# A one-core Nyström attention and SiLU layer: the written-out order of all compute pieces is replaced, and 80 PSUM copies change engine

## The chip, the core and the metric

The kernel runs on one core of a Trainium2 chip. A core has four engines that compute, each with its own queue of instructions that it works off strictly in order: TensorE (PE, matrix products into PSUM; its weight loads are listed apart as PEld), VectorE (DVE), ScalarE (ACT) and GpSimd (POOL). A fifth queue, SyncE (SP), only issues transfers here. An instruction that waits for a semaphore holds up everything behind it in its own queue, and nothing else. Transfers are issued from SP, POOL and, at the very end, ACT, and share the core's 16 DMA engines.

The metric is the time of one execution in microseconds. Three timed runs of the kernel before gave 241.28, 240.32 and 242.66 us, median 241.28.

## The reference

```python
def _attn_ref(q, k, v):                       # (8, 8, 576, 64) each
    q_lm = q.reshape(B, H, 32, 18, D).mean(axis=3)
    k_lm = k.reshape(B, H, 32, 18, D).mean(axis=3)
    A  = sm(q, k_lm)                          # softmax(a @ b.T / 8)
    Bm = sm(q_lm, k_lm)
    C  = sm(q_lm, k)
    Z = Bm.T / (norm_1(Bm) * norm_inf(Bm) + 1e-06)
    for _ in range(6):
        Z = 2 * Z - Z @ Bm @ Z
    return A @ Z @ C @ v

x = attn_out.transpose(0, 2, 1, 3).reshape(4608, 512)
h = x @ w_in                                  # 512 -> 2048
return (h * sigmoid(h)) @ w_out               # 2048 -> 512
```

Landmarks are means over groups of 18 tokens. The inverse of the 32 x 32 matrix Bm is found by six Newton steps, which follow one another. The result is float32.

## The kernel before, in words

The eight batches are worked on one after the other, with two or three of them under way at once. All work is cut into 1,565 named pieces; `name.b` is the piece of batch `b`. A piece is one function that emits one or several instructions on one engine:

- **Loads.** `ldk`, `ld`, `ldv` bring q, k and v; `wi` and `wo` the two weight matrices. The first batch's q and k come through SP and are cast by `kc...ACT` and `kc...DVE`; all other loads go through POOL (lines 398 to 432).
- **Transposed q and k.** For batches 0 to 2 PE transposes (`tr`, line 523) and a copy `trc` takes the block out of PSUM (lines 344 on ACT, 346 on DVE). From batch 3 on SP transposes by DMA (`xt`, line 547). A landmark sum is `lms` on PE for two batches, and `lra` to `lrd` on DVE (line 582) later.
- **Attention.** `sb` and `pb` give Bm; a chain of small DVE pieces and PE products makes the six Newton steps: `ns` (PE), `nsd` (DVE, line 717), `fb` (DVE, line 692), numbered by step and, for batch 0, by half. `A` and `C` are the big score products, each of which fills four PSUM banks; `Ax`, `Cx` are their exponentials on ACT (lines 749, 794), `S`, `Ln`, `Rs`, `etn` the normalisation. `ct` transposes C (by PE with the copy `ctc` for batches 0 and 1, then by DMA on SP, line 821); `cv` multiplies it by v, `wc` scales it (DVE, line 852), `zt` and its copy `ztc` apply Z, and `m0` to `m3` with the copies `mc` carry it through w_in.
- **First layer.** `h0` to `h15` and `hx0`, `hx8` on PE, `g` and `gx` the SiLU on ACT (lines 919, 942).
- **Second layer.** Every tile of 256 tokens is done by seven products of half size instead of eight. A tile's number follows the `@`: 5000 + 100 b + 0 or 20, and 5340, 5740 for the tokens that `gx` collects over four batches. `ss0` to `ss3` (DVE, line 1007) make the sums that the seven products `p1` to `p7` read; `c1`, `u2`, `c5`, `c21` copy a product out of PSUM (ACT or DVE), `c11`, `c12`, `c22` add a second one to it on DVE (line 1042). The first 256 tokens are done plainly (`o`, `oc`). The result lies in one of six staging tiles `ost` until four stores `os` (line 984) have carried it out; the copy that writes a staging tile anew waits for their landing.
- **Filler.** `*n` stands for n matmuls on zeros, 64 in all, in the first 28 us.

What sets the order is a text, `SEQUENCE`, at the head of the file. `Plan.run` goes through its words and each piece is emitted in that place; a word may carry the engine (`c1@5300.0/ACT`) and, behind `<`, the transfer after which it may start (`ld100.5<xt10.4`: those loads wait for that DMA transposition). So the text fixes each engine's queue, and PSUM banks are handed out in the order of the words, from the pieces that freed them. Semaphore waits between queues follow from the data. Nothing is reordered afterwards.

Of the kernel before, what the change touches and what calls it, by code (L numbers as in the profile page):

```python
# [25 lines left out]
Cx10.0 Cx11.0 Cx00.0 pbs.0 pbr.0 bmx.0 bmt.0 csb.0 n1.0 nrm.0 tr09.1 lms000.1 lms006.1 S10.0
lms0012.1 lms010.1 bbd.0 trc09.1/DVE stz.0 f0.0 stf0.0 stf1.0 fb00.0 lms016.1 Ln10.0 S00.0 Ln00.0
fb01.0 lms0112.1 lmc0.1/DVE S01.0 ns00.0 nsd00.0 Ln01.0 S11.0 ns01.0 Ln11.0 nsd01.0 fb11.0 ctm00.0
ctc00.0/DVE tr05.1 trc05.1/ACT tr00.1 trc00.1/ACT Rs1.0 Rs0.0 ns11.0 nsd11.0 fb10.0 fb21.0 tr19.1
trc19.1/DVE ltr0.1 lms100.1 lms106.1 ns10.0 nsd10.0 lms1012.1 tr014.1 lms110.1 lms116.1  # L30
trc014.1/DVE ns21.0 tr114.1 lmT0.1/ACT wi1a wi0a wi1b1 wi1b0 wi3b0 wi3a lms1112.1 lmc1.1/ACT
tr10.1 trc10.1/ACT tr15.1 *2 ltr1.1 lmT1.1/ACT fb20.0 nsd21.0 etn1.0 trc15.1/DVE ns20.0 fb31.0 *3
ns31.0 ctm10.0 trc114.1/ACT etn0.0 nsd31.0 sb.1 pb.1 *1 A.1 Ax01.1 Ax00.1 nsd20.0 fb30.0 pbs.1
wrc.0 *1 ns30.0 nsd30.0 ctc10.0/DVE fb40.0 pbr.1 fb41.0 bmx.1 bmt.1 wi3b1 Ax11.1 Ax10.1 *5 C.1
Cx00.1 Cx11.1 Cx01.1 *1 ns40.0 nsd40.0 ns41.0 nsd41.0 fb50.0 fb51.0 cv0.0 cv1.0 wc.0 S01.1 Ln01.1
ns50.0 nsd50.0 *2 ns51.0 bbd.1 nsd51.0 zbd.0 S11.1 Ln11.1 S00.1 Ln00.1 wi2b0 wi2b1 wi2a ldv0.1
ldv1.1 *5 zt.0 ztc.0/DVE S10.1 ctm00.1 ctc00.1/DVE Rs0.1 Ln10.1 Cx10.1 *2 m1.0 mc11.0/ACT
mc10.0/DVE m0.0 f0.1 mc01.0/DVE mc00.0/ACT *1 ctm10.1 ctc10.1/DVE Rs1.1 csb.1 *1 h4.0 n1.1 m3.0
nrm.1 stz.1 stf0.1 mc31.0/DVE fb00.1 g4.0 mc30.0/DVE h2.0 g2.0 h6.0 g6.0 h0.0 g0.0 h3.0 ns00.1
wrc.1 nsd00.1 fb10.1 h5.0 g5.0 m2.0 mc21.0/ACT mc20.0/DVE *1 h13.0 g13.0 ns10.1 nsd10.1 fb20.1  # L40
h15.0 hx0.0 g15.0 ns20.1 nsd20.1 fb30.1 h9.0 g9.0 h11.0 g11.0 etn0.1 ns30.1 nsd30.1 fb40.1 hx8.0
gx8.0 g3.0 h8.0 h12.0 g12.0 etn1.1 ns40.1 nsd40.1 fb50.1 gx0.0 h10.0 g10.0 ld1.2 tr15.2
trc15.2/DVE h14.0 g14.0 ns50.1 nsd50.1 zbd.1 ldv2.1 cv0.1 wc.1 tr114.2 trc114.2/DVE tr19.2
trc19.2/DVE zt.1 g8.0 ztc.1/ACT tr10.2 trc10.2/DVE lra1.2 h7.0 g7.0 m3.1 mc31.1/ACT mc30.1/ACT
m1.1 mc11.1/DVE mc10.1/ACT h1.0 g1.0 ld0.2 tr00.2 lrb1.2 tr09.2 tr014.2 trc014.2/DVE tr05.2
trc05.2/DVE trc09.2/DVE lrc1.2 trc00.2/ACT h12.1 g12.1 h7.1 g7.1 h15.1 m2.1 mc20.1/ACT m0.1
mc00.1/ACT mc21.1/ACT mc01.1/ACT wo0 o0@5001.0 h14.1 g14.1 g15.1 o0@5000.0 fold lrd1.2 lra0.2
lrb0.2 lrc0.2 lrd0.2 h11.1 g11.1 ltr0.2 ltr1.2 lmT1.2/DVE lmT0.2/ACT ss00@5020.0 ss10@5020.0
ss20@5020.0 ss30@5020.0 wo1 h5.1 o1@5000.0 sb.2 pb.2 pbs.2 pbr.2 bmx.2 bmt.2 wo2 wt00 bbd.2 h8.1
h3.1 o1@5001.0 o2@5000.0 wo3 o2@5001.0 wt01 g8.1 csb.2 o3@5001.0 oc@5001.0/ACT g3.1 g5.1 n1.2  # L50
nrm.2 stz.2 o3@5000.0 hx8.1 f0.2 gx8.1 h0.1 g0.1 oc@5000.0/ACT h2.1 h10.1 g10.1 h4.1 h1.1 g2.1
g1.1 wt11 wt21 stf0.2 fb00.2 ns00.2 h13.1 g13.1 wt31 nsd00.2 fb10.2 wt10 wt20 wt30 p1@5020.0
c1@5020.0/ACT ns10.2 nsd10.2 fb20.2 h9.1 h6.1 g4.1 g9.1 g6.1 ss00@5100.0 p5@5020.0 c5@5020.0/DVE
hx0.1 gx0.1 ss10@5100.0 l1done.0 C.2 Cx00.2 Cx10.2 p6@5020.0 u2@5020.0/DVE ld100.3 ld101.3 ld110.3
ld111.3 ldv1.3 xt10.3<ldv1.3 xt11.3<ldv1.3 ns20.2 nsd20.2 ss20@5100.0 p3@5020.0 c12@5020.0
# [198 lines left out]
def kernel(  # L254
# [9 lines left out]
    nc = tc.nc  # L264
# [86 lines left out]
    A = P.add  # L351
# [817 lines left out]
```

## Time and profile before

| | |
|---|---|
| profiled execution | 242.09 us |
| its span (first to last instruction) | 240.4 us |
| granted TensorE clock, mean | 0.998 |
| PE busy | 231.0 us in 2,948 matmuls |
| DVE busy | 181.7 us in 505 instructions |
| ACT busy | 182.9 us in 436 instructions |
| DMA moved | 37.73 MB, mean 157 GB/s |
| start of the first product on real data | 5.32 us |
| start of the last DVE copy | 236.50 us, 0.42 us long |

The profiled execution took 0.81 us more than the median of the three timed runs. Engines' busy shares are sums over the whole span; a group's mean time is the length of one instruction, and since an engine overlaps the end of one with the start of the next, its step from start to start is shorter (a first-layer SiLU on ACT is 625 ns long and follows the last one after 477 ns).

### The profile page before, as it was taken

The page shows a single profiled execution, that of the slowest core. Times are in us where ns is not written, and L with a number is a line of the kernel's source. Part 1 is how long each engine was busy: PE and PEld are TensorE (multiplying, and loading weights), DVE is VectorE, ACT ScalarE, POOL GpSimd, SP SyncE. Part 2 cuts the span into 40 slices and gives each one's busy share as a digit, 9 for nine tenths or more (in the row PEclk, how much of TensorE's full clock was granted, in tenths as well). Part 3 has the DMA queues.
Part 4 walks back from the last instruction along what each step waited for, and adds up shares of the span by engine and source line. Part 5 has one row for each costly group of instructions (what it writes and reads, how often), then busy time and mean ns, then how long its engine had stood idle before and what let it go on. Part 6 is the DMA issues. An engine that isn't in the chain of part 4 may idle for free.

```text
span 240.4 us, 7520 instructions
## 1 busy us (share of the span) xinstructions
PE 231.0 (96%) x2948; PEld 164.6 (68%) x2948; DVE 181.7 (76%) x505; ACT 182.9 (76%) x436; POOL 49.4 (21%) x89
## 2 busy tenths in 40 slices
PE   6999999999999989999789999999999999999993
PEld 4977556457876645788668655767876665789882
DVE  2679989898998579858699968759898475348762
ACT  3689999989889988998355899999779788634100
POOL 0936842140154006203060352000000000000000
PEclk9999999999999999999999999999999999999999
DMA  6999999999999996998999999992524421012334
GB/s 255 252 205 192 204 211 206 209 205 200 151 176 191 220 216 125 181 190 159 192 166 208 194 186 244 140 209 56 111 60 119 114 57 35 0 44 74 92 108 127
DMA packets 56164, 37.73 MB, mean 157 GB/s; under 512 B 37056, under 2 KB 47552, under 8 KB 56128
## 3 DMA queue, kind: packets, MB, share of 16 engines
q0 software_dynamic: 15168, 17.18, 44.5%
q1 hardware_dynamic: 40144, 19.12, 36.6%
q10 hardware_dynamic: 816, 0.95, 1.4%
q8 instruction: 23, 0.38, 0.6%
q14 instruction: 13, 0.11, 0.2%
HBM read 36.70 MB, written 9.44 MB: 192 GB/s over the span
## 4 chain that ended last, share of the span: by engine, by line
PE 84%; ACT 7%; DMA 2%; SPq 2%; DVE 2%; issue 1%; ACTq 0%; DVEq 0%
PE ps L334 81%; PE ps L523 3%; ACT gm L919 2%; DMA gm<-in_k_dram 2%; ACT L919 1%; SPq L821 1%; ACT L1122 1%; ACT gx L942 1%; SPq L984 1%; ACT m L344 1%; DMA out_dram<-ost 1%; PE ps L809 1%; ACT et L749 1%; DVE ss L1007 0%; DVE ost L1042 0%
## 5 line engine op out<-in xcount | busy, mean ns | idle before, releaser
L919 ACT ACTIVATE gm<-ps 128x512 f16<-128x512 f32 x128 | 68.7, 625 | 8.4 <-PE ps L334 7.9
L334 PE MATMUL ps<-etn,m 128*128 128x512 bf16 (+1 forms) x512 | 72.0, 286 | 0.2
L334 PEld LDWEIGHTS <-gm 128*128 128x128 f16 x512 | 48.5, 98 | 12.7 <-issue 1.6
L334 PE MATMUL ps<-w_out_sb,gm 128*128 128x256 f16 (+1 forms) x392 | 53.1, 281 | 0.1
L334 PEld LDWEIGHTS <-ss 128*128 128x128 f16 x408 | 39.2, 98 | 10.8 <-issue 2.8
L334 PEld LDWEIGHTS <-m 128*128 128x128 bf16 x512 | 31.1, 98 | 20.1 <-issue 2.1
L334 PE MATMUL ps<-wt,ss 128*128 128x256 f16 x272 | 34.6, 273 | 0.4 <-DVE st L717 0.4
L1042 DVE TENSOR_TENSOR ost<-ost,ps 128x256 f32<-128x256 f32 x51 | 21.0, 417 | 15.8 <-PE ps L334 8.1
L344 ACT COPY ost<-ps 128x256 f32<-128x256 f32 (+1 forms) x45 | 17.2, 388 | 12.3 <-PE ps L334 9.8
L344 ACT CAST m<-ps 128x512 bf16<-128x512 f32 x36 | 19.4, 613 | 1.8 <-PE ps L334 1.6
L415 POOL DMA_DIRECT2D v<-in_v_dram x24 | 14.5, 616 | 27.6 <-PE ps L334 25.2
L346 DVE CAST m<-ps 128x512 bf16<-128x512 f32 x28 | 18.3, 685 | 2.2 <-PE ps L334 1.9
L717 DVE SCALAR_TENSOR_TENSOR st<-st,ps 128x128 bf16<-128x128 bf16 (+2 forms) x54 | 13.6, 257 | 8.1 <-PE ps L334 4.8
L334 PE MATMUL ps<-w_out_sb,ss 128*128 128x256 f16 x136 | 17.5, 273 | 1.4 <-ACT ost L344 1.4
L398 POOL DMA_DIRECT2D qk<-in_k_dram x20 | 10.5, 546 | 35.6 <-DMA qT<-qk 17.7
L334 PE MATMUL ps<-wt,gm 128*128 128x256 f16 x120 | 15.6, 273 | 0.0
L759 ACT ACTIVATE ln<-ps 128x288 f32<-128x288 f32 x32 | 12.4, 415 | 3.7 <-PE ps L334 3.2
L692 DVE TENSOR_TENSOR fb<-st,hmask 128x256 bf16<-128x256 bf16 (+1 forms) x54 | 14.4, 272 | 1.0
L398 POOL DMA_DIRECT2D qk<-in_q_dram x20 | 10.5, 543 | 21.3 <-issue 11.9
L794 ACT ACTIVATE ce<-ps 128x288 bf16<-128x288 f32 x32 | 13.0, 424 | 2.5 <-PE ps L334 2.3
L1007 DVE TENSOR_TENSOR ss<-gm 128x1024 f16<-128x1024 f16 x15 | 10.2, 686 | 5.2 <-ACT gm L919 5.2
L749 ACT ACTIVATE et<-ps 128x288 bf16<-128x288 f32 x32 | 11.1, 423 | 2.9 <-PE ps L334 2.9
(93 smaller groups left out, 345.0 us busy)
## 6 DMA issues: line engine op xcount, KB each, us to landing
out_dram<-ost SPq DMA_DIRECT2D x128, 64.0 KB, 2.2
v<-in_v_dram POOLq DMA_DIRECT2D x24, 192.0 KB, 7.3
qk<-in_k_dram POOLq DMA_DIRECT2D x20, 144.0 KB, 5.9
qk<-in_q_dram POOLq DMA_DIRECT2D x20, 144.0 KB, 6.8
w_out_sb<-in_moe_w_out_dram POOLq DMA_DIRECT2D x4, 512.0 KB, 15.0
gm<-in_k_dram SPq DMA_DIRECT2D x2, 576.0 KB, 4.2
gm<-in_q_dram SPq DMA_DIRECT2D x2, 576.0 KB, 6.5
qk<-in_q_dram POOLq DMA_DIRECT2D x2, 576.0 KB, 8.2
```

The costliest lines, as they stand in the source:

```text
L334: nc.tensor.matmul(out=out_ap, lhsT=lhsT, rhs=rhs, start=start, stop=stop, skip_group_check=True)
L344: nc.scalar.copy(out=out, in_=in_)
L346: nc.vector.tensor_copy(out=out, in_=in_)
L398: lambda e, t=t, g=g, h=h, src=src: nc.gpsimd.dma_start(out=qk_r[b % 2][64 * h:64 * h + 64, t, g].rearrange("p j d -> p (j d)"), in_=src[b ...
L415: lambda e, a=a: nc.gpsimd.dma_start(out=v_r[b % 2][a * L:(a + 1) * L, :, :], in_=v[b].rearrange("h (l a x) d -> a l h (x d)", l=L, a=VA)[ ...
L692: nc.vector.tensor_tensor(out=fb[it % 2][:, g0:g1], in0=bc(sr[it % 3][:, g0:g1, 0:L], 4, 2), in1=bc(hmask, n, 1), op=OP.mult), [o], 14.5 + ...
L717: nc.vector.scalar_tensor_tensor(out=s2[:, g0:g1, lo:SW], in0=s[:, g0:g1, lo:SW], scalar=2.0, in1=ps[:, 0:NG * SW].rearrange("p (g x) -> p ...
L749: lambda e, g=g, et=et, c=c: nc.scalar.activation(out=et[:, c], in_=bank(me["A"], 2 * g + c)[:, 0:HS], func=AF.Exp, scale=sc / J),
L759: lambda e, g=g, c=c, ln=ln: nc.scalar.activation(out=ln[:, c], in_=bank(me["S", g, c])[:, 0:HS], func=AF.Ln),
L794: nc.scalar.activation(out=ce[:, :, 0:VP].rearrange("p (i c) (a l) -> p c a i l", c=2, a=VA)[:, c], in_=bank(me["C"], 2 * g + c)[:, 0:HS]. ...
L919: lambda e, dc=dc, cell=cell: nc.scalar.activation(out=gm[:, dc, :], in_=bank(cell["o"]), func=AF.Silu),
L1042: nc.vector.tensor_tensor(out=out_, in0=x, in1=y, op=OP.add)
```

## The change

`SEQUENCE` is written anew. It holds the same 1,565 pieces and the same 64 filler matmuls. The transfers of SP, of POOL and of ACT stand in the same order as before within their queues, and the words behind `<` are the same. All compute pieces may stand elsewhere, and 80 of the copies that either DVE or ACT can do have changed engine: 45 from ACT to DVE (13 `mc`, 13 of `c1`, `c5` and `c21`, 6 `u2`, 5 `lmT`, 3 `trc`, 3 `ztc`, one `lmc`, one `oc`) and 35 the other way (11 of `c1`, `c5` and `c21`, 9 `mc`, 5 `trc`, 3 `u2`, 2 each of `lmc`, `lmT` and `ztc`, one `ctc`). Since transfers wait for the last word that wrote their data, the compute pieces that some transfers wait for differ as well. Two lines outside the text let a store hand back its instruction; nothing uses it in this order. The diff, cut to the places that are spoken of below (first the old text, then the new one):

```diff
-ldk10 ldk11 ldk00 ldk01 const ident kc10ACT kc10DVE kj10 *15 lms100.0 tr15.0 tr10.0 trc10.0/DVE
...
-lmT0.0/ACT *6 sb.0 pb.0 trc014.0/DVE trc09.0/DVE A.0 Ax01.0 Ax00.0 Ax10.0 Ax11.0 *5 C.0 Cx01.0
...
-etn0.2 lmT0.3/ACT sb.3 c12@5100.0 c21@5020.0/ACT p7@5100.0 pb.3 pbs.3 pbr.3 fb50.2 A.3 Ax11.3
...
-zbd.2 zt.2 ztc.2/ACT S10.3 Ln10.3 p4@5100.0 Cx11.3 ss00@5120.0 c11@5100.0 os@5100.0 ss10@5120.0
...
-ns50.3 nsd50.3 zbd.3 h11.2 g11.2 h13.2 h3.2 cv0.3 wc.3 g4.2 g13.2 g3.2 etn1.3 zt.3 ztc.3/DVE
...
-ss20@5300.0 pbs.5 Ln00.4 p4@5220.0 p5@5300.0 c21@5220.0/ACT c5@5300.0/ACT Rs0.4 pbr.5 ss30@5300.0
-bmx.5 nsd00.4 fb10.4 wrc.4 p6@5300.0 u2@5300.0/ACT p3@5300.0 csb.5 ns10.4 n1.5 ss00@5320.0 etn1.4
...
-Ax10.5 Ax00.5 c1@5320.0/ACT p5@5320.0 ss10@5320.0 ns30.4 ss20@5320.0 ss00@5340.0 f0.5 stf0.5
-p4@5300.0 Ax01.5 Ax11.5 S11.5 Ln11.5 c21@5300.0/ACT p6@5320.0 u2@5320.0/ACT nsd30.4 fb40.4 ns40.4
...
+ldk10 const ident kc10DVE *1 kc10ACT ldk11 kc11DVE *1 ldk00 ldk01 kc11ACT *2 kc00ACT kc01ACT *1
...
+trc19.0/DVE tr15.0 trc15.0/ACT A.0 Ax01.0 ltr0.0 lmT0.0/DVE *1 Ax11.0 Ax10.0 *1 ld1.2 sb.0 pb.0
...
+etn1.0 ctc10.0/ACT lmc1.1/DVE nsd20.0 trc19.1/DVE trc10.1/ACT nsd11.0 trc014.1/DVE *1 ltr1.1
...
+Rs1.3 mc31.2/DVE c12@5100.0 etn1.3 ldv2.4<xt00.3 u2@5120.0/ACT os@5100.0 bbd.3 Cx01.3 os@5101.0
...
+ns50.3 h1.2 h3.2 cv0.3 ldv1.5 nsd50.3 g1.2 g14.2 etn0.3 wc.3 zbd.3 h0.2 hx0.2 zt.3 h2.2 g0.2 g3.2
...
+p5@5300.0 S00.4 Ln00.4 nsd00.4 ss20@5320.0 p6@5300.0 pbs.5 fb10.4 c5@5300.0/DVE ns10.4 nsd10.4
+p2@5220.0 fb20.4 ss00@5340.0 c1@5320.0/ACT ns20.4 S01.4 ct1.4<ldv1.5 p3@5300.0 c21@5220.0/ACT
...
-        {"SP": nc.sync, "ACT": nc.scalar}[e].dma_start(
+        return {"SP": nc.sync, "ACT": nc.scalar}[e].dma_start(
...
-            o.ins = getattr(r, "ins", None)
+            o.ins = getattr(r[-1] if isinstance(r, list) else r, "ins", None)
```

More of the change, by code (lines that the diff above doesn't have):

```diff
@@ L26 @@
[L26 to L55, printed above, removed]
@@ new lines @@
+ld110.6 c12@5320.0 ld111.6 p1@5340.0 nsd10.5 c21@5300.0/ACT c1@5340.0/ACT m1.4 mc11.4/ACT fb20.5
+ct0.5<ldv1.6 m3.4 mc30.4/ACT ldv0.5<xt00.4 mc31.4/DVE c11@5340.0 p4@5320.0 ns20.5 mc10.4/ACT
+etn1.5 m2.4 m0.4 mc00.4/DVE c21@5320.0/ACT ss30@5340.0 mc01.4/ACT p6@5340.0 h2.4 ct1.5<ldv1.6
+h12.4 h7.4 nsd20.5 mc20.4/DVE fb30.5 mc21.4/ACT h14.4 ns30.5 h8.4 g7.4 ldv2.5<xt00.4 g12.4 h10.4
+etn0.5 g10.4 h9.4 h5.4 h4.4 u2@5340.0/DVE g8.4 g2.4 p5@5340.0 nsd30.5 g9.4 wrc.5 fb40.5 ns40.5
+g14.4 xt00.6<ldv1.6 cv0.5 ldv0.7<xt00.6 ss10@5340.0 g5.4 h6.4 g6.4 nsd40.5 fb50.5 ns50.5 hx0.4
@@ L157 @@
+p7@5740.0 os3@5721.0/SP os0@5721.0/SP os1@5721.0/ACT os0@5720.0/ACT ss30@5740.0 os2@5721.0/ACT
+c22@5740.0 p3@5740.0 c12@5740.0 os11@5740.0/ACT os13@5740.0/SP os12@5740.0/ACT os10@5740.0/SP
+p4@5740.0 c21@5740.0/DVE os3@5741.0/ACT os2@5741.0/SP os1@5741.0/ACT os0@5741.0/SP
 """
```

219 lines of the change are left out of this document (121 added, 98 removed).

## The prediction

> **What bounds the kernel now.** I read the page's busy shares, then the chain that ended last, then the table of waits, and then the queues of PE, ACT and SP around each wait that PE has.
>
> ```profile
> PE 231.0 (96%) x2948; PEld 164.6 (68%) x2948; DVE 181.7 (76%) x505; ACT 182.9 (76%) x436; POOL 49.4 (21%) x89
> ...
> PE 84%; ACT 7%; DMA 2%; SPq 2%; DVE 2%; issue 1%; ACTq 0%; DVEq 0%
> ```
>
> PE is busy for 96% of the span and makes up 84% of the chain. Both orders give PE the same products, so only its waits, and what lies before its first and after its last product, can change. I therefore measured every piece by two numbers. Its **position** is the sum of the steps (start to start, without waits) of all PE work ahead of it: a product 512 wide takes 216 ns, one 256 wide 109 ns (the 16 of 1.91 us below). All positions together make 219.4 us in either order, 7.0 of it the early fillers. Its **lag** is its start in the trace less its position: what PE has lost so far. In the trace of before the lag is 1.1 at the first filler, 4.1 at `A.0` (start 12.14), 6.3 at `m0.0` (26.23), 8.1 at 60 us, 9.2 at 88, 10.4 at 90, 12.2 at `p3@5300` (117.70), 13.4 at 128, 14.4 at 140 and 16.9 from 200 on. After PE's last product 4.1 us follow to 240.4, and 1.7 lie around the span (242.09). So the order can win or lose in some 17 us of lag, much of it small change between products; waits that a name stands for are few.
>
> ```profile
> ACT ost L344 <- DMA out_dram<-ost: 2.0, 1, 2.0
> PE ps L334 <- ACT ost L344: 1.4, 1, 1.4
> PE ps L334 <- ACT qk L344: 0.9, 1, 0.9
> PE ps L334 <- DVE wsb L852: 0.7, 1, 0.7
> ```
>
> Columns: total us, times, longest. The largest wait of PE in mid-kernel is one copy of ACT into a staging tile, and that copy waited for a store. The three queues show the chain (start, length, idle before):
>
> ```profile
> 72.15 5.08 SPq L984 DMA_DIRECT2D out_dram<-ost  x8
> 78.39 2.54 SPq L821 DMA_TRANSPOSE ct<-ce  x2
> 81.04 6.94 SPq L547 DMA_TRANSPOSE qT<-qk  x4
> 88.03 4.79 SPq L984 DMA_DIRECT2D out_dram<-ost  x8
> 101.76 5.94 SPq L547 DMA_TRANSPOSE qT<-qk  x4
> 107.79 7.63 SPq L984 DMA_DIRECT2D out_dram<-ost  x12
> ...
> 117.28 0.37 ACT L344 COPY ost<-ps 128x256 f32<-128x256 f32 x1 [1.98 <-DMA out_dram<-ost]
> ...
> 114.44 1.91 PE L334 MATMUL ps<-wt,ss 128*128 128x256 f16 x16
> 117.70 1.03 PE L334 MATMUL ps<-w_out_sb,ss 128*128 128x256 f16 x8 [1.35 <-ACT ost L344]
> ```
>
> PE stops from 116.3 to 117.7. It waits for the PSUM bank that `c5@5300` empties on ACT; that copy waits for the staging tile of store `os@5121`, which landed at 117.18. SP issued that store late because its queue was late: the stores of 107.79 stand behind four transpositions, which began when the loads behind them had landed, and those loads are gated by the four transpositions of 81.04. The store chain thus sets PE's time at 117 us, whatever was won before.
>
> **The change part by part.**
>
> *Engines of 80 copies.* A 128x512 cast takes 613 ns on ACT and 685 on DVE, a 128x256 copy 373 and 415. By steps the queues go from 168.5 to 165.4 us (ACT) and from 162.9 to 166.2 (DVE); neither is near 219. I cost the move as a whole at nothing and its places below. The cover is thin where an engine is full:
>
> ```profile
> core 0: us, PE busy (x) PEld busy (x) DVE busy (x) ACT busy (x) POOL busy (x), PEclk, DMA share, GB/s
> 20.00:40.00 20.00, 19.92 (x350) 11.71 (x351) 18.38 (x62) 19.34 (x47) 10.63 (x17) 1.00 1.21 206
> ```
>
> *Opening (to 60 us).* The first q cast is earlier: `A.0` can start about 11.15 (last cast ends 9.88, a transposition 0.28, a copy 0.72, waits between) instead of 12.14. Between the first exponential and the start of SiLU ACT has 15.2 us of steps in the new order against 14.3 plus 1.5 idle, so it reaches SiLU at 27.0 to 28.5 (before: 28.22). The loads don't move: part of w_in lands at 29.60 and lets `m2.0` begin, v lands at 36.0 for `cv0.1`; with the new positions this allows lags no lower than 6.5 and 7.05 there (before 6.9 and 7.5). I take -0.5 at 60 us, from -1.0 (the whole of `A.0`) to +0.4 (ACT at its late end).
>
> *At 87 us.* `wc.3` now has other work between it and `cv0.3`, so PE's wait of 0.66 (and the weight load's part, 0.82 in all) goes.
>
> *The SP chain.* In before SP issues `os@5100` at 72.15, after `c11@5100`; in the new order the last writer is `c12@5100`, moved behind `mc31.2`, and ready at about 76.6: 4.5 later. Behind it in SP's order stand eight stores (0.47 each, to 80.6), two transpositions (2.54; start 78.39 before, so +2.2), and four of q and k. These four took 6.94 because the first lasted 2.63, until the loads of v at 83.38 were in; the others took 1.3 to 1.4. Started after those loads they take 4 x 1.4, say 5.8: end at 89.0 against 87.98. Before, the gated loads behind them could start when they had landed, 2.0 to 3.7 after their end (at 91.69); so the shift of the chain is between -0.7 and +1.0, or as much as the 4.5 in the worst case (a rival). I take +0.1, near the middle.
>
> *At 117 us.* So all that was won before (0.5 and 0.82) is swallowed: PE comes to this place at about 115.9 and waits. But the wait is another one. `c5@5300` is now on DVE and waits for the same landing (117.2 + 0.1); behind it in DVE's queue stand `nsd10.4` and `fb20.4`, for which `ns20.4` on PE waits. It starts at 117.38 + 0.33 + 0.2 + 0.2, about 118.2 with the semaphores, at position 106.35: lag 11.85, against 12.16 before at `p3@5300`, so **-0.3** with the +0.1 in it. ACT stands too: `c1@5320` waits for the landing of `os@5200` (118.46 before) from 116.1 on. That is 2.3 us of ACT that before lay elsewhere; SiLUs behind it feed PE, and before, the exponentials had 5 us of slack there. I price this at nothing and at up to +1.
>
> *From 118 us on.* Before, PE still loses 4.7 us of lag. Of its waits with a cause these go: `nsd10.4` 0.16, `nsd20.4` 0.52, `stf0.5` 0.42, and six small ones, 1.3 together (`h2.4` 0.24, `p6@5400` 0.26, `p1@5500` 0.24, `p1@5520` 0.16, `p5@5520` 0.17, `h9.6` 0.24): -2.4. In the new order I find pieces whose source comes fewer PE steps ahead than the source's own time: `m2.4` 0.20, `h3.4` 0.26, `h10.5` 0.29, `p1@5520` with `h14.6` 0.29, `h11.6` 0.17, `p7@5320` 0.10: +1.3, and I allow 0.4 for what I did not see. Sum **-0.7**, from -2.0 (no new one shows) to +0.8 (they come twice as large).
>
> *Tail.* `p4@5740` is the last product at the same position in both, followed by the same copy and four stores: 4.1 us, unchanged.
>
> **Sum.** -0.3 - 0.7 = **-1.0 us**. On the profiled execution 242.09 becomes 241.1; that execution is 0.81 above the median of the runs, so the forecast is **240.3 us** (-0.4%). Its own range is 236.9 to 243.4: below, the rest at -2.0, the chain's landing early by 0.7 and half the store gain of the next paragraph; above, +0.9 from the chain, +1 from ACT and the upper end of the rest.
>
> **Rivals.**
>
> *The store lands as stores do.* `os@5121` took 4 to 7 us from issue to landing because the gated loads (issued 110.1 to 112.2) shared the DMA engines; the stores' table gives 1.5, 2.0 and 7.0 as least, median and most. If, in the new order, that store is issued before those loads press, c5 does not wait, the opening's 0.5 and `wc.3`'s 0.8 survive and some 0.7 more of the 1.5: -3.0 in all on the profiled basis, **238.3**. For it: 2.0 is the median. Against: the order of SP and the gates are the same, and stores and loads come out of one chain, so they shift together. 0.26.
>
> *The late store is passed down (slower).* SP works strictly in order. If the two transpositions and the four behind them take as long as before although they start later, the 4.5 us of `os@5100` reach the gated loads, the transpositions of 101.76 and the stores of 107.79 nearly whole, and PE's stop at 117 grows by as much: it decides when the four end at 91.4 or later rather than at 89.0 (shift 3.5 or more). It costs 4.4 - 0.3 at 118, less what the rest gives back: +3.3, or **244.6**. For it: those transpositions lasted 6.94 and 5.94 in the two places that show; nothing after 88 us leaves SP more than a gap of 8.9 us, and that gap is itself the wait for the loads. Against: the first of the four plainly waited for other transfers, 2.63 against 1.35. 0.27.
>
> *The clock falls.* The start shows fillers of 213 ns where the same product later takes 109, and the clock at 1.00 through PE's stop of 1.4 us at 116. Should the stop at 117 grow past what the clock stands, PE would run the following 3 us at half speed, +1.6 on top of a stop that is longer by 1 to 2: **243**. 0.04. The Trainium skill ("TensorE: Matmul & The Clock Gate", Part 1: The HAM clock gate) says that an idle window of about 3.4 us halves the clock, and as long a busy one brings it back. The trace agrees with half speed at the start; no stop of that length is in the trace of before.
>
> *The change doesn't do what it says.* Excluded as far as the programs go: transfers stand in the same order and gates in each queue; but the pieces that a store waits for are others, which is the case above.
>
> **How the numbers follow.** 240.3 with 0.43; faster rival 0.26; late chain 0.27; clock 0.04. The range that should hold 8 in 10 reaches to the faster case's lower side and the late chain's price: 236.8 to 245.0. About 1% (2.4 us) is what a measurement of this kernel can tell from no change. Faster by over 1% (below 238.9): most of the faster case and a little of the forecast's low side, 0.30. Slower by over 1% (above 243.7): most of the late chain, the upper side of the clock, 0.28. Within: 0.42.
>
> **What would show it.** Right: `A.0` near 11.2; lag about 7.6 at 60 us; no wait for wsb at 87; the four transpositions ending near 89; a wait of PE of about 2 us near 116 whose releaser is DVE (`ns20.4`); a lag near 11.8 there and near 15.9 after 200. Wrong: transpositions ending past 91, or the stores of 107.79 starting past 110 (late chain); no wait over 0.5 near 116 (faster); a clock below 0.95 between 100 and 125. What would upset all of it: waits of ACT in the first 40 us, where its 19.34 of 20 leaves nothing to hide a copy that I have placed too early.

## The result: 0.75% slower

| | before | after |
|---|---|---|
| median of 11 runs each | 241.97 us | 243.47 us (242.85 to 244.96) |
| ratio of the times, 95% interval | | 1.0075 (1.0046 to 1.0103) |
| profiled execution | 242.09 us | 243.02 us |
| its span | 240.4 us | 241.3 us |
| lag at 60 us / at 104 us of position / at the end | 8.1 / 10.6 / 16.9 us | 9.2 / 13.7 / 17.9 us |

The forecast was 240.3 us with a range of 236.8 to 245.0. The time lies in the range, and within 1% of before, but it moved the other way, and the interval leaves no doubt of the direction. It lies in the range only because that was drawn up to the price of the rival "late store is passed down"; the forecast's own range ended at 243.4. The two profiled executions differ by 0.9 us, the two medians by 1.5, and the ratio of 1.0075, which is used from here on, means 1.8. The profiled execution of the new order is among its three fastest runs, so the traces show a little less than the whole.

The page of the new order, the busy shares and the chain that ended last:

```profile
PE 231.9 (96%) x2948; PEld 163.8 (68%) x2948; DVE 185.4 (77%) x515; ACT 179.7 (74%) x426; POOL 49.3 (20%) x89
...
PE 71%; DMA 13%; ACT 4%; SPq 4%; DVE 3%; issue 2%; POOL 1%; DVEq 0%; POOLq 0%
```

PE does the same work. But PE's share of the chain has gone from 84% to 71%, and DMA's from 2% to 13%: the chain runs for longer stretches through transfers than before. The table of waits of the new order (total us, times, longest) names them:

```profile
ACT ost L344 <- DMA out_dram<-ost: 4.8, 2, 3.1
PE ps L334 <- DVE rs L582: 1.6, 2, 0.8
PEld L334 <- DVE rs L582: 1.4, 2, 1.1
```

The old stop at `c5@5300` and the wait for `wsb` are gone from PE's rows. In their place PE waits for `rs`, the last step of the landmark sums (`lrd`), whose input is what SP has transposed. The queue of SP in the new order (start, length):

```profile
65.73 16.25 SPq L984 DMA_DIRECT2D out_dram<-ost  x16
83.74 2.54 SPq L821 DMA_TRANSPOSE ct<-ce  x2
86.39 6.25 SPq L547 DMA_TRANSPOSE qT<-qk  x4
92.69 3.94 SPq L984 DMA_DIRECT2D out_dram<-ost  x8
104.91 5.67 SPq L547 DMA_TRANSPOSE qT<-qk  x4
110.68 7.31 SPq L984 DMA_DIRECT2D out_dram<-ost  x12
```

The two transpositions start at 83.74 instead of 78.39, the four at 86.39 instead of 81.04, the next four at 104.91 instead of 101.76. The stores `os@5100`, inside the row of 16, went out at 78.36 (72.15 before) and landed by 84.58 (79.81). And PE at the place where those transpositions are needed, the new order again:

```profile
112.46 0.28 PE L334 MATMUL ps<-rs,fold 128*128 128x256 f16 x1 [0.85 <-DVE rs L582]
...
115.21 0.27 PE L334 MATMUL ps<-rs,fold 128*128 128x256 f16 x1 [0.72 <-DVE rs L582]
...
120.74 0.23 PE L334 MATMUL ps<-st,fb 128*128 128x64 bf16 x2 [0.49 <-DVE fb L692]
```

Where the lag comes from, by position, old order and new:

```
position      8     12     16     20     28     44     60     76     80     92    104    112    128   end
before      4.10   4.97   5.54   6.30   7.37   8.04   8.26   9.15  10.41  10.43  10.64  13.00  14.24  16.88
after       4.69   4.99   6.14   7.27   8.06   9.12   9.35  10.92  11.22  11.62  13.73  14.59  15.30  17.88
```

The opening loses 1.1 (position 12 to 44), the stretch from 60 to 76 loses 0.7, leaving out the wait for `wsb` brings 1.0 back at 78, the landmark sums cost 1.9 at 100 to 104, and from there on the new order is 2.1 better, since the old stop at 117 and several small waits are not in it. What stays is 1.0. This table can't say which of these are causes: a loss may be swallowed by a later wait, and an opening of the same instructions varies (below). Hence the experiments.

### The profile page after: what moved, and what is told of

It is laid out like the page before. It is cut to its first block, busy times and chain, and to the rows that moved or that the text cites. A ratio compares the mean times of both kernels' runs of the same rounds, so it can differ in the third digit from the quotient of the medians.

```text
span 241.3 us, 7511 instructions
## 1 busy us (share of the span) xinstructions
PE 231.9 (96%) x2948; PEld 163.8 (68%) x2948; DVE 185.4 (77%) x515; ACT 179.7 (74%) x426; POOL 49.3 (20%) x89
## 4 chain that ended last, share of the span: by engine, by line
PE 71%; DMA 13%; ACT 4%; SPq 4%; DVE 3%; issue 2%; POOL 1%; DVEq 0%; POOLq 0%
PE ps L334 68%; DMA ct<-ce 3%; DMA qk<-in_q_dram 3%; DMA qT<-qk 3%; DMA gm<-in_q_dram 3%; PE ps L523 2%; SPq L547 2%; DMA out_dram<-ost 2%; SPq L984 2%; DVE ss L1007 1%; POOL qk L398 1%; ACT m L344 1%; ACT gm L919 1%; PE ps L809 1%; ACT L919 1%
## 5 line engine op out<-in xcount | busy, mean ns | idle before, releaser
L919 ACT ACTIVATE gm<-ps 128x512 f16<-128x512 f32 x128 | 67.7, 639 | 6.1 <-PE ps L334 5.8
L344 ACT COPY ost<-ps 128x256 f32<-128x256 f32 (+1 forms) x39 | 14.5, 384 | 16.6 <-PE ps L334 11.1
L346 DVE CAST m<-ps 128x512 bf16<-128x512 f32 x32 | 20.9, 682 | 3.3 <-PE ps L334 3.3
L415 POOL DMA_DIRECT2D v<-in_v_dram x24 | 14.5, 618 | 33.6 <-PE ps L334 29.4
L344 ACT CAST m<-ps 128x512 bf16<-128x512 f32 x32 | 17.4, 596 | 3.1 <-PE ps L334 3.0
L346 DVE COPY ost<-ps 128x256 f32<-128x256 f32 (+1 forms) x31 | 13.0, 427 | 8.2 <-PE ps L334 6.2
L398 POOL DMA_DIRECT2D qk<-in_k_dram x20 | 10.5, 546 | 35.2 <-DMA qT<-qk 18.3
L942 ACT ACTIVATE gx<-ps 128x512 f16<-128x512 f32 x16 | 10.0, 626 | 9.7 <-PE ps L334 9.7
L398 POOL DMA_DIRECT2D qk<-in_q_dram x20 | 10.5, 550 | 20.9 <-issue 12.4
```

Of the source, the lines that this page charges most:

```text
L344: nc.scalar.copy(out=out, in_=in_)
L346: nc.vector.tensor_copy(out=out, in_=in_)
L398: lambda e, t=t, g=g, h=h, src=src: nc.gpsimd.dma_start(out=qk_r[b % 2][64 * h:64 * h + 64, t, g].rearrange("p j d -> p (j d)"), in_=src[b ...
L415: lambda e, a=a: nc.gpsimd.dma_start(out=v_r[b % 2][a * L:(a + 1) * L, :, :], in_=v[b].rearrange("h (l a x) d -> a l h (x d)", l=L, a=VA)[ ...
L919: lambda e, dc=dc, cell=cell: nc.scalar.activation(out=gm[:, dc, :], in_=bank(cell["o"]), func=AF.Silu),
L942: lambda e, d0=d0, cell=cell, c=c: nc.scalar.activation(out=gx[:, d0:d0 + 8, c:c + 64], in_=bank(cell["o"]).rearrange("p (c x) -> p c x", ...
```

## The experiments

All ratios are against the order before, timed on the same chip. Not all kernels were timed on one chip, so two of them are compared by their ratios. The length of a stop of PE is given from the start of the product ahead of it to the start of the one that waited; the idle times in brackets in the profile lines are 0.1 to 0.3 us less.

| run | what it is | ratio (95%) |
|---|---|---|
| (after) | the new order | 1.0075 (1.0046 to 1.0103) |
| open_new | new to 60 us, then old | 1.0067 (1.0035 to 1.0099) |
| open_old | old to 60 us, then new | 1.0038 (1.0003 to 1.0073) |
| middle_new | new from 60 to 133 us alone | 1.0114 (1.0069 to 1.0159) |
| engines_new | old order, new engines | 1.0957 (1.0919 to 1.0995) |
| order_new | new order, old engines | 252.84 us against 242.31, one run |
| new_c12_early | new, one copy moved forward | 1.0004 (0.9976 to 1.0033) |
| old_c12_late | old, that copy late, stores not | 1.0110 (1.0054 to 1.0165) |
| old_chain_late | old, that copy late, stores too | 1.0164 (1.0102 to 1.0225) |
| new_gate_ct0 | new, one gate changed | 1.0071 (1.0026 to 1.0115) |
| early_cv_late | new_c12_early, two products moved | 0.9961 (0.9916 to 1.0005) |
| early_ct_dve | new_c12_early, two copies on DVE | 1.0037 (0.9999 to 1.0075) |
| new_c5_behind | new, one copy moved back | 1.0053 (1.0014 to 1.0092) |
| old_wsb_gone | old, `zt.3` later | 0.9985 (0.9952 to 1.0018) |
| old_open_c12_early, _b, _c | old to 60 us, then new with the copy forward | 0.9972 (0.9942 to 1.0001), 0.9962 (0.9921 to 1.0003), 0.9975 (0.9944 to 1.0006) |
| new_mended | early_cv_late with two more edits | 0.9987 (0.9961 to 1.0012) |

### Which stretch

The text was cut into stretches. Since transfers stand in the same order in both texts, a stretch of one can be followed by what is left of the other. The seam of `open_new` (the words up to `p7@5020` are the new ones):

```diff
 ... p3@5020.0 p1@5100.0 c12@5020.0 ct1.2<ldv1.3 oc@5001.0/ACT p7@5020.0
-A.2 Ax01.2 ct0.2<ldv1.3 nsd20.2 fb30.2 ss00@5120.0 ss20@5100.0 ss30@5100.0 ...
+kj11 kj01 kj00 l1done.0 nsd20.2 ss20@5100.0 l1done.1 A.2 Ax01.2 Ax10.2 ...
```

> The new order up to its 459th piece (about 60 us), the old order for all that is left. Theory 'opening': in the traces the lag is 1.08 larger in the new order at 60 us (9.34 against 8.26), ACT has 1.0 more to do before its SiLU table and reaches it at 28.84 instead of 28.25, and the final difference is that same 1.0; so this run is slower than before by 1.0 us (0.6 to 1.5), ratio about 1.004. Rival 'store chain': what is lost before 60 us is swallowed by the stop of 1.6 us at p3@5300, which stores and loads set, and the result is that of before (within 0.3 us).

Measured 1.0067, 1.6 us. The rival ("swallowed") falls: what the opening loses is not taken up at 117. The stop at `p3@5300` was there all the same, and longer (PE from 118.20 to 120.17).

The seam of `open_old`:

```diff
 ... ld011.3 xt01.3<ldv1.3 xt00.3<ldv1.3 ldv0.2 ldv2.2 ldv1.2
+l1done.3 l1done.2 Cx01.2 Cx11.2 p1@5100.0 ct1.2<ldv1.3 A.2 Ax01.2 ct0.2<ldv1.3 fb30.2 ...
```

> The old order up to its 459th piece (about 60 us), the new order for all that is left. 'Opening': all of the loss goes, the time is that of before within 0.4 us, ratio 1.000 (0.998 to 1.002). 'Store chain': the late os@5100 and the stops at 111 to 120 us stay, the loss stays, ratio 1.005 or more.

Measured 1.0038: by the middle of the runs half of the loss goes (0.37%, 0.9 us) and half stays. The interval overlaps that of the new order, so the half is an estimate. Neither theory alone gives this. The trace shows the stops of the new order, each longer: 1.28 at `ltr1.5`, 1.70 at `ltr0.5`, 0.93 at `ns20.4`, against 1.04, 0.99 and 0.76.

`middle_new` goes back to the old text behind the 1,032nd piece:

```diff
 ... l1done.3 l1done.2 Cx01.2 Cx11.2 p1@5100.0 ... ld111.7 wc.5 zt.5 ldv2.6<xt00.5
+h3.4 g3.4 ztc.5/ACT xt10.6<ldv1.6 xt11.6<ldv1.6 lra1.6 lrb1.6 m2.5 ...
```

> The old order up to 60 us and from about 133 us on (1,032 pieces), the new one between. 'Opening': lag over this stretch grew by 6.8 in the new order and by 6.7 in the old, so the time is that of before, within 0.4 us. 'Store chain': slower by 1.0 to 1.5 us, ratio 1.004 to 1.006.

Measured 1.0114, 2.8 us. So "opening" is not the only cause: the middle costs by itself, which is what "store chain" said, and more than it said. 1.33 of its lag arises at `m2.5` (144 us), close behind the seam; the seam may have made that itself.

### Engines and order

`engines_new` keeps the old order and gives the 80 copies the new engines; `order_new` is the other half.

```diff
-lmT0.0/ACT ... mc31.2/ACT ... c5@5300.0/ACT ...
+lmT0.0/DVE ... mc31.2/DVE ... c5@5300.0/DVE ...
```

> The old order with the engines of the new one (80 copies moved, nothing else). 'Opening': ctc10.0 and ztc.0 put 0.96 us more on ACT between 12 and 29 us, where it has nothing to spare, so slower by 0.5 to 1.2 us, if no other of the 78 costs anything. 'Store chain': engines matter little, 0 to 0.4 us. If each copy has been fitted to its own order, the old order could also lose more, 1.5 to 3 us.

Measured 1.0957, 23 us. Waits are spread over the whole span: 2.04 at `p6@5120` for `c1@5120`, 1.61 at `ltr0.2`, 1.41 at `p3@5740`, and some forty smaller ones.

```diff
-lmT0.0/DVE ... mc31.2/DVE ... c5@5300.0/DVE ...
+lmT0.0/ACT ... mc31.2/ACT ... c5@5300.0/ACT ...
```

> The new order with the old engines of the 80 copies. Theory 'fitted': each choice of engine belongs to its own order, as engines_new showed for the old one (+9.6%), so slower by 4 to 12% here too, with waits of PE for copies over the whole span. Rival 'engines alone': the new set of engines is the poorer one whatever the order, and the time is that of before or better.

252.84 against 242.31, 10.5 us slower. "Fitted" holds: each choice of engine belongs to its place in its own order. Neither half of this change can be priced by itself.

### The late store

```diff
-... mc31.2/DVE c12@5100.0 etn1.3 ...
+... p4@5100.0 c12@5100.0 S11.3 ...
```

> The new order with one piece moved: c12@5100 stands directly behind p4@5100 again, so that its store os@5100 can be issued near 74 instead of 78.4. Theory 'store landing': the transposition ct1.3 waits for the landing of these stores (83.66 in the new order, 78.31 in the old), so it starts near 80 instead of 83.7, the gated loads near 93 instead of 95.2, and PE's two waits for landmark sums at 111 and 115 us (0.9 each) shrink to under 0.5 together; 0.8 to 2.0 us faster than the new order, so 0 to +1.0 against before. Rival 'opening only': the stop only moves elsewhere, and the time stays at that of the new order (+1.8, ratio about 1.0075).

Measured 1.0004: of the 1.8 us that the new order is slower, this one word takes back 1.7, and the two intervals don't meet. The queue of SP in this kernel:

```profile
80.50 2.55 SPq L819 DMA_TRANSPOSE ct<-ce  x2
83.16 7.22 SPq L545 DMA_TRANSPOSE qT<-qk  x4
90.44 4.38 SPq L982 DMA_DIRECT2D out_dram<-ost  x8
103.13 6.46 SPq L545 DMA_TRANSPOSE qT<-qk  x4
```

`os@5100` went out at 73.56 and its first part landed at 76.70 (83.66 in the new order, where `ct1.3` followed at 83.74). The transpositions started at 80.50, and what lets them go is now another thing: ACT's exponentials `Cx10.3`, which they transpose, end at 80.38. These too stand later in the new order (79.88; 72.48 in the old). So with the first wait gone the chain starts 3.2 us earlier, and the exponentials hold it there. The later four started at 103.13 instead of 104.91. PE's stop at `ltr1.5` is gone, the one at `ltr0.5` is 0.59 long instead of 0.99. The lag grows by 0.6 from position 96 to 104 instead of 2.0. The earlier copy also frees its PSUM bank earlier (73.53, not 78.33), which is a rival for the gain; but from position 60 to 96 the growth of the lag in the two traces differs by 0.3 only, so what was won was won at the landmark sums. In this execution the opening was worse (8.08 at `m0.0`) and the lag at the end still 0.5 smaller than in the new order's trace.

The same the other way round, in the old order:

```diff
-... lmT0.3/ACT sb.3 c12@5100.0 c21@5020.0/ACT ...
+... c1@5120.0/ACT p6@5120.0 u2@5120.0/DVE c12@5100.0 mc01.2/ACT ...
```

> The old order with one piece moved: c12@5100 stands behind u2@5120, where DVE reaches it near 77.5, so that os@5100 is issued some 5.5 us later than in the old order. 'Store landing': ct1.3 starts near 83, the gated loads 2 to 3 us later than 92.3, and PE's stop at p3@5300 grows by about as much; since the last part of the old order has no slack either (middle_new lost 1.3 at m2.5), slower by 2 to 3.5 us, ratio 1.008 to 1.014. 'Opening only': the chain has slack, within 0.5 us of before.

In this kernel `os@5100` stands ahead of `c12@5100` in the text, so the store leaves without the sum that `c12` adds: half of the columns of 128 tokens lack one product. And the store is not late (72.21). The 1.1% is therefore not what was asked for: the product's PSUM bank is held until 80.59 instead of 68.8, later pieces get other banks, DVE waits for the store's landing (80.05) before it can add, and from position 60 to 72 PE falls 3.6 us behind the old order, in many waits. Of this 3.5 are left at 84 and 2.0 at the end: the stop at `p3@5300`, 1.6 us in the old order, does not occur. Here a loss was swallowed, as `open_new` did not show. The next kernel moves the stores behind the copy too:

```diff
-... Cx11.3 ss00@5120.0 c11@5100.0 os@5100.0 ss10@5120.0 ... c21@5100.0/ACT os@5101.0 ct1.3<ldv1.4 m2.2 ...
+... u2@5120.0/DVE c12@5100.0 os@5100.0 os@5101.0 ct1.3<ldv1.4 mc01.2/ACT ...
```

> The old order with c12@5100 behind u2@5120 as in old_c12_late, and os@5100, os@5101 and ct1.3 behind it in the text, so that the stores wait for c12@5100 (near 77.5) and DVE for nothing. 'Store landing': as expected there, ct1.3 starts near 83, the gated loads 1.5 to 3 us later than 92.3, slower than before by 2 to 3.5 us, ratio 1.008 to 1.014. 'Slack': ratio below 1.003.

Measured 1.0164; `ct1.3` at 84.99, the gated loads at 96.89 (92.27 before). The bank's price is in both kernels, so their difference is an estimate of the chain's: 0.5%, 1.3 us by the middle of the ratios, whose intervals overlap (in the two traces 2.7 at position 106, 4.0 at the end). In this kernel `ct1.3` follows the stores ahead of it in SP's queue at once, when the first part of `os@5100` has long landed (83.73): the late issue alone holds it. So for the new order `new_c12_early` shows that the late `os@5100` costs some 1.7 us. That it costs about as much in the old order is likely, not shown.

### The gate of four loads

In the new order `ct0.2` was issued at 64.39 and landed at 71.53, and PE stopped for it (0.46 over its step). The chain that ended last, around there:

```profile
63.85 0.54 issue
64.39 7.14 DMA ct<-ce
71.58 13.85 PE ps L334 x189
```

```diff
-ld100.4<xt00.3
+ld100.4<ct0.2
```

> The new order with one gate changed: the four loads ld100.4 to ld111.4 wait for the landing of the transposition ct0.2 instead of that of xt00.3. Theory 'collision': in the new order these loads are issued at 64.0, 0.4 us ahead of ct0.2, which then lands 7.1 us after its issue (2.7 in the old order, where the loads come 1 us behind it). So ct0.2 lands near 67, cv0.2 no longer stops PE (0.46), loads start near 67 and still land ahead of the transpositions of 86 us; 0.3 to 0.7 us faster than the new order at 72 us. Later loads may take part of it. Rival: ct0.2 is late because of the stores behind it, and lands near 71 again.

`ct0.2` was issued at 64.88 and landed at 67.39; the four loads went out at 67.97 instead of 64.01, and the stop at `cv0.2` is gone. So "collision" holds for the transposition. In time it brings nothing: 1.0071. `os@5100` waits for `c12@5100` as before and goes out at 78.54, and the stops at 111 to 121 us add up to 3.1 instead of 2.8. What is won ahead of the late store is lost behind it.

### The opening

In the new order's trace PE stops between two products of `cv1.0`, and no semaphore explains it. The queue of PE in `new_c12_early`, where the stop is longest:

```profile
20.55 0.38 PE L332 MATMUL ps<-v,ct 96*32 96x64 bf16 x25
21.92 0.35 PE L332 MATMUL ps<-v,ct 96*32 96x64 bf16 x23 [1.00 <-issue]
```

```diff
-trc114.1/ACT cv0.0 cv1.0 fb21.0 sb.1 pb.1 A.1 Ax11.1
+trc114.1/ACT fb21.0 sb.1 pb.1 A.1 cv0.0 cv1.0 Ax11.1
```

> As new_c12_early, with cv0.0 and cv1.0 behind A.1 instead of ahead of sb.1. In the traces PE stops at its 705th or 706th instruction, at 20.6 to 22.5 us, with no semaphore to wait for: 0.51 to 1.31 us in the four runs that open with the new order, 0 to 1.27 in the five with the old; 16 KB on the queue named instruction land at 19.8 to 21.0, some 1.4 us ahead of its going on. Theory 'code': the new order comes to that instruction too early, through the 48 small products of cv0.0 and cv1.0. With these behind A.1 the stop shrinks by 0.5 us or more, S00.1 follows earlier, and the lag at m0.0 is near 6.9 to 7.3 instead of 8.08; ratio to before 0.997 to 0.999. Rival 'ACT': the exponentials keep their times, the stop is replaced by a wait for Ax00.1, lag 7.8 or more, ratio 1.000.

Measured 0.9961, against 1.0004 without the edit; lag 7.30 at `m0.0` instead of 8.08. The stop is gone; `sb.1` now waits 0.6 for copies, and then all of it runs through (queue of PE in `early_cv_late`):

```profile
20.06 0.39 PE L521 MATMUL ps<-idb,qk 128*128 128x128 bf16 x4
20.82 0.20 PE L332 MATMUL ps<-lmT 64*32 64x32 bf16 x5 [0.37 <-DVE qT L344]
...
21.22 0.60 PE L332 MATMUL ps<-v,ct 96*32 96x64 bf16 x48
```

"Code" named the place of the stop, and the stop went. The size is not shown. The intervals of the two kernels overlap, and a lag near 7.3 at `m0.0` is no sign of the edit: the new order itself and `open_new`, which open with the same words without the edit, have 7.27 and 7.26 there. Over all traces, at position 44, the five openings with the new words and engines as they were have on average 1.2 us more lag than the nine with the old words and engines, the two with this edit 0.6 more. That favours "code" for about half of what the opening loses; the rest is open, and "ACT" (a ratio of 1.000) is not excluded by the interval.

```diff
-ctc10.0/ACT ... ztc.0/ACT
+ctc10.0/DVE ... ztc.0/DVE
```

> As new_c12_early, with ctc10.0 and ztc.0 on DVE as in the old order, which takes 0.96 us of steps off ACT between 12 and 29 us. 'ACT': SiLU starts 0.6 to 0.9 us earlier and the lag from 28 us on is 0.6 to 0.9 smaller, ratio to before 0.997. 'Code': ACT has an idle wait of 0.43 between the two, so only ztc.0's 0.27 can count; lag 0 to 0.3 smaller, or larger if DVE is now late; ratio 1.000.

1.0037: not faster. `m1.0` now waits 0.48 for `ztc.0` behind DVE's queue, and the lag at 28 us is 9.03 against 8.88. "ACT" is not borne out: SiLU's table comes at 29.80 against 29.65. The new wait may hide a part of it, so it isn't excluded either. In this profile `ct0.2` took until 73.72 and PE stopped 1.79 for it; that is the collision again.

### The copy on DVE, and the wait for wsb

```diff
-fb10.4 c5@5300.0/DVE ns10.4 nsd10.4 p2@5220.0 fb20.4 ss00@5340.0
+fb10.4 ns10.4 nsd10.4 p2@5220.0 fb20.4 c5@5300.0/DVE ss00@5340.0
```

> The new order with c5@5300 moved behind nsd10.4 and fb20.4 on DVE. Theory 'held up': c5@5300 waits for the landing of os@5121 (119.62 in the new order) and holds those two, so that PE's stop of 0.65 at ns20.4 is its doing; it goes, and p3@5300, which waits for c5@5300, is late next, since the landing is the same: 0 to 0.6 us faster than the new order, ratio to before 1.005 to 1.0075. Rival: no stop follows, and the whole 0.7 is gained.

The stop at `ns20.4` is gone and stands one product further on, where the landing of `os@5121` (121.28 here) lets `c5@5300` go (queue of PE in this kernel):

```profile
121.25 0.29 PE L332 MATMUL ps<-et,hmask 128*128 128x288 bf16 x1
121.88 1.03 PE L332 MATMUL ps<-w_out_sb,ss 128*128 128x256 f16 x8 [0.35 <-DVE ost L344]
```

1.0053 is within the interval of the new order. "Held up" names the mechanism rightly, and it is worth nothing that can be measured, because the landing is the limit.

```diff
-cv0.3 wc.3 g4.2 g13.2 g3.2 etn1.3 zt.3 ztc.3/DVE etn0.3 p3@5120.0
+cv0.3 wc.3 g4.2 g13.2 g3.2 etn1.3 etn0.3 p3@5120.0 zt.3 ztc.3/DVE
```

> The old order with zt.3 and ztc.3 behind p3@5120, so that wc.3 has two products' time. The wait for wsb at 87 us goes (0.82). Theory 'swallowed': loads and stores keep their times, PE comes 0.8 earlier to p3@5300 and waits 0.8 longer there; within 0.3 us of before. Rival 'kept': the whole chain behind moves 0.8 earlier, ratio 0.9966.

Inconclusive. The wait for `wsb` went, but `m3.3` now follows `zt.3` at once and waits 1.57 for `ztc.3`; the stop at `p3@5300` shrank to 0.91. The time is that of before.

### Both causes left out

```diff
 (open_old)
-... mc31.2/DVE c12@5100.0 etn1.3 ...
+... p4@5100.0 c12@5100.0 S11.3 ...
```

> The old order up to about 60 us, the new order for the rest, with c12@5100 directly behind p4@5100. 'Store landing' together with 'opening': this leaves both causes out and keeps what the new order has behind 60 us, the removed wait for wsb (0.8) and the later cv0.5; against before 0 to -2.0 us, ratio 0.992 to 1.000. 'Opening only': as open_old, ratio 1.004.

0.9972, and the queue of SP is back near the old times (`ct1.3` again directly behind `Cx10.3`, 78.65):

```profile
78.77 2.55 SPq L818 DMA_TRANSPOSE ct<-ce  x2
81.42 7.17 SPq L544 DMA_TRANSPOSE qT<-qk  x4
88.64 4.71 SPq L981 DMA_DIRECT2D out_dram<-ost  x8
100.94 6.43 SPq L544 DMA_TRANSPOSE qT<-qk  x4
```

Against the new order's 1.0075: the old opening gives 0.0037 (`open_old`), the early copy 0.0071 (`new_c12_early`), both 0.0103. The two add up to the whole within the intervals. The second is a cause, followed from its word to PE's stops; the first is a stretch, and what in it costs the time is only known in part.

Two followers. `_b` moves `zt.2` behind `sb.3`, and `ltr0.5` with its copy behind `p1@5300`; `_c` moves `zt.2` alone:

```diff
-wc.2 zt.2 S00.3 sb.3 ...        lrd0.5 ltr0.5 lmT1.5/ACT f0.4 ... p1@5300.0 ...
+wc.2 S00.3 sb.3 zt.2 ...        lrd0.5 lmT1.5/ACT f0.4 ... p1@5300.0 ltr0.5 lmT0.5/ACT ...
```

> As old_open_c12_early, with zt.2 behind sb.3 (PE waited 0.36 for wc.2) and ltr0.5 with its copy behind p1@5300 (PE waited 0.90 for lrd0.5). Both waits go; of the 1.2 us some comes back where sb.5 is now later. 0.3 to 1.0 us faster than old_open_c12_early; against before -0.8 to -2.0 us, ratio 0.992 to 0.997. Rival: PE's next stop (c5@5300 and nsd10.4, which the stores set) takes it all, ratio 0.997.

> As old_open_c12_early, with zt.2 behind sb.3 alone (PE waited 0.36 for wc.2 there). If the two causes found are the ones that matter, 0.5 to 1.5 us faster than before, ratio 0.994 to 0.998, with the interval below 1. If not, ratio 0.999 to 1.001, and all that can be said is that leaving both out brings the new order back to the old one.

0.9962 and 0.9975. `_b` was expected 0.3 to 1.0 us ahead of `old_open_c12_early` and came 0.2 ahead by the ratios; the interval of `_c` was expected to lie below 1 and reaches 1.0006. In `_b` the wait for `lrd0.5` went and two others came, 0.94 at `f0.4` and 0.74 at `sb.5`. Last, `early_cv_late` with the gate and the moved copy:

```diff
-ld100.4<xt00.3 ... fb10.4 c5@5300.0/DVE ns10.4 nsd10.4 p2@5220.0 fb20.4
+ld100.4<ct0.2  ... fb10.4 ns10.4 nsd10.4 p2@5220.0 fb20.4 c5@5300.0/DVE
```

> early_cv_late with two more edits: ld100.4 to ld111.4 wait for the landing of ct0.2 (as in new_gate_ct0), which takes away the stop of 0.49 at cv0.2, and c5@5300 behind nsd10.4 and fb20.4 (as in new_c5_behind), which takes away the stop of 1.04 at ns20.4 or gives it to p3@5300. Against early_cv_late 0 to 1.5 us faster; against before 1.0 to 2.4 us faster, ratio 0.990 to 0.996.

0.9987, where 0.990 to 0.996 was expected. The stop at `cv0.2` went; the one at `ns20.4` moved to `p3@5300` (0.97). No further gain over `early_cv_late`.

So none of these versions is shown to beat the order before: five kernels lie between 0.996 and 0.999, and each interval reaches 1 or a little more. Each is shown to beat the new order as it was.

## Why the prediction was wrong, step by step

**What bounds the kernel** was read rightly in so far as the chain through SP decides: the new order loses most where PE needs what that chain brings. That all that was won ahead of 117 us is swallowed there is not borne out: `open_new` showed a loss that was not swallowed, and for a gain `old_wsb_gone` decided nothing.

**Engines of 80 copies at nothing.** As a whole the queues came out as counted (ACT 179.7 busy, DVE 185.4, PE's work unchanged). But "an edit of engines" does not exist apart from the order: alone it costs 9.6%.

**Opening, -0.5.** This step failed; by the ratios the opening costs +0.9 (`open_old`) to +1.6 (`open_new`). First, the gain was no gain: `A.0` started at 11.36, as foreseen (11.15), but at a lag of 4.13 against 4.10. It had only been moved to an earlier position. The step compared two times of a piece where the working had laid down that lags are to be compared. Second, the loads, the copies and ACT were taken as all that can hold PE up; the stop of 0.5 to 1.3 us for code was not among them. It shows in the trace of before, too, as 0.49 at 15 us within `f0.0`, and was read there as small change. In the new order's trace it is 0.55 at `cv1.0`, so between these two traces it makes no difference. Third, SiLU's table came at 28.84, past the range of 27.0 to 28.5. In three traces of the new opening with stops of 1.1 to 1.3 us (`new_c12_early`, `new_c5_behind`, `new_gate_ct0`) ACT stood 1.0 to 1.2 us behind the stop and the table came at 29.4 to 29.9. But with the stop gone it still came at 28.87 (`early_cv_late`) and 28.52 (`new_mended`): part of the delay has another cause, which stays open.

**At 87 us, 0.82.** Right: the lag grows by 0.3 there instead of 1.3.

**The SP chain, +0.1.** This is the step that cost most. The late store was seen, and its issue sized at 4.5 us late (6.2 came, 1.3 of it by the lag that PE had by then). But the transpositions were started as soon as the stores behind it had been issued, at 80.6. The landing of `os@5100`, which the step put at nothing, held them: its first part took 5.3 us, from 78.36 to 83.66. SP's own waits show it, in the new order and in the old:

```profile
SPq L821 <- DMA out_dram<-ost: 1.6, 1, 1.6
SPq L821 <- DMA out_dram<-ost: 1.1, 1, 1.1
```

`ct1.3` reads nothing that the store writes, so no data call for the wait. The trace's semaphore records show where it comes from. SP's transfers use eight semaphores in turn, and each waits for the landing of the transfer that used its semaphore before: in both orders that is, for 149 of the 159 such waits, the one eight places ahead in the queue, be it a store or a transposition. The first part of `os@5100` stands eight places ahead of `ct1.3`. Also the exponentials that `ct1.3` reads, which had been ready 5 us ahead in the old order (`Cx11.3`, the later one there, at 73.44), were ready at 79.9 only; no step asked for them. The old queue held the hint: there is a gap of 1.16 ahead of `ct1.3`, issued at 78.39, and in the trace the first part of `os@5100` lands at 78.31. The gap was not asked for its cause.

The four transpositions ended at 92.6 and not at 89.0. Of these 3.6 us the later issue is 1.4 (the stores were through at 82.0, not 80.6), the wait for the landing 1.7, and the length of the four 0.5 (6.25, not 5.8). So the point at which the rival "late store is passed down" decides (91.4) was passed. That rival, at 0.27, is what happened in outline, but the wait for the landing is not among its reasons. Of 5.35 us at `ct1.3`, 4.7 were left at the end of the four, 2.9 at the gated loads, where +0.1 was forecast, since the landing behind the four took 2.0 us instead of 3.7, and 3.2 at the next transpositions. The rival's price of +3.3 is about twice the 1.5 to 1.8 that came.

**At 117 us, -0.3.** The new wait is the one foreseen: `ns20.4` on `fb20.4`, behind `c5@5300` and the landing of `os@5121`; `new_c5_behind` confirms it. But PE was held up twice before that, 1.0 each at `ltr1.5` and `ltr0.5`, which read what `lrd1.5` and `lrd0.5` make of the transpositions issued from 104.91 on. These two were not in the sum. The late landing has a helper in them, the new order of DVE (its queue in the new order):

```profile
109.79 0.69 DVE L582 TENSOR_TENSOR red<-qT 128x1024 f16<-128x1024 bf16 x1 [1.59 <-DMA qT<-qk]
110.40 0.68 DVE L1007 TENSOR_TENSOR ss<-gm,ss 128x1024 f16<-128x1024 f16 x1
111.00 0.41 DVE L1042 TENSOR_TENSOR ost<-ost,ps 128x256 f32<-128x256 f32 x1
111.34 0.74 DVE L582 TENSOR_TENSOR red<-red 128x512 f16<-128x512 f16 x2
112.11 0.29 DVE L582 TENSOR_TENSOR rs<-red,qT 128x256 f16<-128x256 f16 x1
```

`lra1.5` starts as the transposition lands, but `ss30@5220` and `c22@5200` stand between it and `lrb1.5`, 0.86 us, and four small pieces between `lrb0.5` and `lrc0.5`, 0.81; in the old order the four steps of each sum follow one another at once. `new_c12_early` has the same order on DVE and no stop at the first place, 0.6 at the second. So landing and order on DVE make these stops together; no run moves those pieces alone. Lag at `ns20.4`: 14.4 instead of 11.8.

**From 118 us on, -0.7.** Right in sign: from position 110 to the end 3.4 instead of 4.6 in the two traces, -1.2, inside the range that was given. With both causes left out the new order is 0.25 to 0.4% faster than the old by the middle of the runs, which is near the sum of -1.0 us for an order without them, but partly by luck, since the opening's -0.5 in that sum was wrong; the intervals don't exclude nothing. **The range.** Its upper end adds up to 243.7 (240.3 and 0.9, 1 and 1.5), not 243.4; nothing hangs on it.

**Tail.** Right: 4.9 us from the start of `p4@5740` to the end of the span, 5.0 before. **Clock.** The granted clock stayed at 1.00 from 100 to 120 us, and the longest stop of PE behind the opening was 2.0 us in any run (`engines_new`). The Trainium skill ("TensorE: Matmul & The Clock Gate", Part 1: The HAM clock gate) says that an idle window of about 3.4 us halves the clock; no stop was as long, so no run here tests it.

## What to carry to other kernels

When an order is rewritten and the transfers keep theirs, ask of each transfer which compute piece is now the last it waits for, and follow it to the landing, not to the issue: where a queue's transfers share a few semaphores in turn, as SP's share eight here, a late store can hold up a transposition that reads nothing of it, and the loads behind that. A gap in a queue that no data explain is worth asking for its cause. Compare pieces by what the engine has lost up to them, not by their start: a piece that comes earlier because it was moved forward has gained nothing. That a gain ahead of such a chain counts only if the chain's own start moves with it is argued, not shown: `old_wsb_gone`, at 0.9985, neither bears it out nor excludes it.

## What the runs showed of the hardware

**PE stops for its program.** The queue named instruction brings 16 KB 23 times in an execution. In the opening, with loads at 200 GB/s beside it, PE stopped with no semaphore at its 705th or 706th instruction, in all seven traces that open with the new order's words as they were (0.36 to 1.31 us), in neither of the two in which `cv0.0` and `cv1.0` had been moved, and in two of the ten that open with the old ones (0.40 in `middle_new`, 0.46 in `old_open_c12_early_b`). Two more of the ten stop there, for 1.27 (`open_old`) and 1.30 (`old_wsb_gone`); for these the profile names a wait for ACT, which had ended 0.2 us before PE went on. `before`, `old_chain_late` and `new_c5_behind` stopped at the 450th, for 0.49, 0.60 and 0.96. The second of these 16 KB landed between 19.8 and 21.0 us, and PE went on 1.3 to 1.5 us after that in all eleven. In none of the 19 traces does PE start its 224th, 352nd or 480th product (instructions 448, 704 and 960, as each product has one weight load) sooner than 1.2 us after the first, second or third packet has landed. What the profile's view of the DMA queues says of the new order from 18 to 20 us:

```profile
q0 software_dynamic: 322, 0.30, 112.3%
q8 instruction: 1, 0.02, 3.0%
```

The single packet of 16 KB stands beside 322 of the loads. Stops without a semaphore also occur at the 961st instruction (0.30 to 0.73 us in the old openings); 450, 706 and 961 lie 255 or 256 apart, 16 KB for 256 would be 64 bytes each, and 23 times 256 is 5,888, where PE has 5,896 instructions. That the stop is a wait for code is inferred from these places, from the times, and from `early_cv_late`; no view names it.

**The same opening is not the same each time.** Kernels with identical instructions up to 60 us had lags from 6.0 to 7.4 us at `m0.0` with the old words, 7.3 to 8.4 with the new. The stop goes with it: among the old openings the two with stops of 1.27 and 1.30 have 7.4, the other seven 6.0 to 6.9. A single profile can't tell openings apart by less than a microsecond; repeated timings had to.

**An earlier load can make a transposition later.** `ct0.2` took 6.5 to 8.8 us to land in the six traces in which `ld100.4` and the three loads with it were issued 0.3 to 1.4 us ahead of it, 2.7 to 4.8 where they came 0.5 to 2.8 us behind it, and 2.5 and 2.9 where they waited for it.
